# Query loads in 1-KB rows, first casts moved to ScalarE and VectorE, spare transposes in the waits of the ramp, and a new order of work

## The chip, the cores and the metric

One Trainium2 chip, one core of it. The time is device microseconds (us) of the program's execution on that core. A kernel is run several times; medians with the range are given, and a verdict rests on runs of the chip's fast state alone. A ratio is the mean time of one kernel's fast runs over the mean of the other's fast runs in the same rounds on the same chip, so it is not quite the ratio of the two medians that are quoted. In what follows PE is TensorE, DVE is VectorE, ACT is ScalarE, POOL is GpSimd and SP issues most of the DMAs. PSUM holds what TensorE puts out; all other tiles of the kernel lie in SBUF. The ramp is the first part of the run, in which TensorE is not yet full. A string is a row of GpSimd's instructions with no gap between them.

## The reference

Two parts in a row. First linear attention with a decay per head, over blocks of 64 tokens (batch 4, 8 heads, 768 tokens, head size 64). Then a gated MLP whose gate mixes tokens:

```python
for b in range(nb):                                   # 12 blocks of 64 tokens
    intra = einsum('bhic,bhjc->bhij', qb, kb) * Dmask
    out_b = einsum('bhij,bhjd->bhid', intra, vb) + einsum('bhid,bhde->bhie', qb * lam_pow, kv_state)
    kv_state = lam_block * kv_state + einsum('bhsd,bhse->bhde', kb * rev_pow, vb)
x = out as [B, S, H*D]
h = maximum(x @ w_in, 0);  u, v = halves of h
v_n = (v - mean) / sqrt(var + 1e-06)                  # per token
v_s = einsum('ts,bsd->btd', w_spatial, v_n) + b_spatial
out = (u * v_s) @ w_out
```

## The kernel before

The work is cut into 12 tiles of 256 tokens, three to a batch entry. Every tile goes through loads of q, k, v (512-byte rows), casts to bf16 (`kd`, `qc`, `vc`), transposes on TensorE into one PSUM tile `pt` (tiles 0 to 7; later tiles by DMA), copies out of it (`kT` on ScalarE, `qT` on VectorE with the query decay), scores `pam`, a mask `a`, products `pkv` for the state `s`, the output `pat`, and a copy `xT` of it on ScalarE. A batch entry then has `pv` (normalised to `vn` by VectorE), `pu`, `pvs`, `h`, the gate `gT`, and `po`.

Parts that matter here:

```python
    def cast_k(n):
        cast(n, "k", "kd", ldec, nc.gpsimd)
    def cast_v(n):
        s["vc"] = att.tile([P, H, 2, D], BF16, tag="vc", name=f"vc_{n}")
        nc.gpsimd.tensor_copy(out=s["vc"], in_=s["v"])
    def copy_qT(n):
        nc.vector.tensor_tensor(out=transposed(n, "qT"), in0=st[n]["pt"][:, 1],
                                in1=lq[:, n % NR].rearrange("p m g x -> p (m g) x"), op=ALU.mult)
    # ... cut ...
    def copy_x(n):
        # ... cut ...
        nc.scalar.activation(
            out=xT[b][:, r].rearrange("p c g (d m) -> p (c g) m d", m=2),
            in_=st[n]["po"].rearrange("p c g (m d) -> p (c g) m d", m=2), func=AF.Copy)
    # ... cut ...
    def norm(b, r):
        # ... cut ...
        for t in (2 * r, 2 * r + 1):
            nc.vector.tensor_scalar(out=vn[:, t, :], in0=gm["vh", b][:, t, :],
                                    scalar1=mv[:, t, 0:1], scalar2=rstd[:, t:t + 1],
                                    op0=ALU.subtract, op1=ALU.mult)
```

Every engine runs its instructions in the order in which one long string names them. `T:4` is the transposes of tile 4, `vn:1:0` the normalisation of the first pair of token blocks of batch entry 1, `g:0:0` a gate, `cv:6` the cast of v of tile 6, and so on:

```python
    order = """
        q:0 q:1 k:0 k:1 v:0 q:2 k:2 k:3 v:1 v:2 q:3 v:3 ld:0 cq:0 q:4 lq:0 cq:1 lq:1 ck:0 k:4
        lq:2 ck:1 k:5 T:0 qT:0 T:1 kT:0 qT:1 cq:2 kT:1 A:0:0 A:0:1 cv:0 wv v:4 q:5 a:0:0 K:0
        ... (26 further lines)
```

## Time and profile before

| | before |
|---|---|
| time, median of the first 3 runs | 158.95 us (158.13 to 158.96) |
| profiled span | 156.3 us |
| busy: PE, DVE, ACT, POOL | 85%, 60%, 50%, 50% |
| DMA | 51,987 packets, mean 196 GB/s |

The prediction below shows the slices and stretches. What it does not show are three groups that the outcome turns on. These are groups of instructions of the kernel before by line and form: operation, out<-in, sizes, count | busy us in all, mean ns of one | idle time of the engine before them.

```profile
L308 ACT ACTIVATE xT<-pat 128x1024 bf16<-128x1024 f32 x12 | 15.7, 1322 | 9.8 <-PE pat L299 9.8
L352 DVE TENSOR_SCALAR vn<-vh,mv,rstd 128x512 bf16<-128x512 bf16 x24 | 13.3, 596 | 0.4
L205 DVE TENSOR_TENSOR qT<-pt,lq 128x1024 bf16<-128x1024 bf16 x8 | 5.5, 691 | 14.4 <-PE pt L191 9.7 <-ACT kT L202 4.7
```

The mean of `vn` (596 ns) hides two kinds: most take about 410 ns, a few over a microsecond. In the time order of VectorE, a pair of them normally takes 0.73 us, and the longest pair of this kernel 2.42:

```profile
34.56 0.73 DVE L352 TENSOR_SCALAR vn<-vh,mv,rstd 128x512 bf16<-128x512 bf16 x2
41.43 2.42 DVE L352 TENSOR_SCALAR vn<-vh,mv,rstd 128x512 bf16<-128x512 bf16 x2
```

(Start, duration, engine, instruction.) VectorE had begun the second pair and took 1.7 us longer over it, while GpSimd ran a cast of k (`kd`, 41.45 us, 1.93 long). Another pair, at 126.15 us, took 2.12 beside a gate.

### The profile page before, as it was taken

To read this page: it belongs to the slowest core of one execution; us is meant where nothing else is said; L and a number is where in the kernel's file an instruction comes from. 1 tells how busy PE (TensorE), PEld (TensorE's weight loads), DVE (VectorE), ACT (ScalarE), POOL (GpSimd) and SP (SyncE) were. 2 spreads that over 40 slices of the span, in tenths; PEclk is the share of its full clock that TensorE was granted. 3 is DMA by queue.
4 is the path that set the end of the run, shared out by engine and by line. 5 is a ranking of instruction groups with operands and counts; after the bars stand their busy time and mean duration, and the time that the engine had idled before them with its cause. 6 is when DMAs were issued, how large, how long until landed. Compare 5 with 4: busy or idle time off the path is not lost.

```text
span 156.3 us, 4534 instructions
## 1 busy us (share of the span) xinstructions
PE 132.8 (85%) x1992; PEld 88.7 (57%) x1992; DVE 94.0 (60%) x167; ACT 78.0 (50%) x103; POOL 77.7 (50%) x63
## 2 busy tenths in 40 slices
PE   0009469989989999989899999999999999999970
PEld 0008469646868667836665567665665557646440
DVE  1401975696967958656982874787395976424510
ACT  3896234564869423546555033658543376022360
POOL 4076966720359299799802059937220066470000
PEclk9999965999999999999999999999999999999996
DMA  2999999999998999994596995991890011006085
GB/s 43 305 291 290 290 247 295 246 261 212 260 271 260 269 277 204 296 292 124 143 294 115 229 244 125 180 268 31 259 256 33 0 72 66 0 0 268 10 319 208
DMA packets 51987, 30.70 MB, mean 196 GB/s; under 512 B 9472, under 2 KB 48896, under 8 KB 51968
## 3 DMA queue, kind: packets, MB, share of 16 engines
q1 hardware_dynamic: 49312, 27.53, 68.3%
q0 software_dynamic: 2368, 2.75, 10.5%
q8 instruction: 15, 0.25, 0.7%
q10 hardware_dynamic: 288, 0.14, 0.3%
q14 instruction: 4, 0.03, 0.1%
HBM read 24.78 MB, written 6.29 MB: 199 GB/s over the span
## 4 chain that ended last, share of the span: by engine, by line
PE 57%; DMA 16%; SPq 9%; ACT 8%; DVE 4%; POOL 3%; issue 1%; POOLq 0%; ACTq 0%
PE pvs L371 20%; PE po L409 12%; DMA k_in<-in_k_dram 11%; PE pv L325 9%; SPq L72 9%; PE pu L360 8%; DMA v_in<-in_v_dram 5%; ACT wt_sb L461 3%; PE pat L299 2%; ACT vh L330 2%; POOL kd L165 2%; PE pt L191 2%; PE pam L227 1%; ACT kT L202 1%; ACT uT L365 1%
## 5 line engine op out<-in xcount | busy, mean ns | idle before, releaser
L235 DVE TENSOR_TENSOR a<-pam,causal 128x1024 bf16<-128x1024 f32 x24 | 28.7, 1219 | 9.2 <-PE pam L227 9.1
L371 PE MATMUL pvs<-wt_sb,vn 128*128 128x384 bf16 x192 | 32.9, 326 | 0.3 <-ACT wt_sb L461 0.2
L397 POOL TENSOR_TENSOR gT<-h,uT 128x768 bf16<-128x768 f32 x12 | 19.6, 1644 | 21.6 <-PE po L409 16.1
L165 POOL TENSOR_TENSOR kd<-k_in,ldec 128x1024 bf16<-128x1024 f32 x12 | 23.3, 1944 | 12.0 <-DMA k_in<-in_k_dram 11.2
L371 PEld LDWEIGHTS <-vn 128*128 128x128 bf16 x192 | 18.4, 98 | 12.3 <-issue 0.2
L360 PE MATMUL pu<-xT,win_sb 128*128 128x256 bf16 x192 | 22.6, 273 | 0.0
L325 PE MATMUL pv<-win_sb,xT 128*128 128x512 bf16 x96 | 22.3, 380 | 0.0
L386 DVE TENSOR_TENSOR h<-pvs,bsp_bc 128x768 f32<-128x768 f32 (+1 forms) x17 | 15.3, 904 | 11.4 <-PE pvs L371 11.4
L431 ACT ACTIVATE o<-po 128x1024 f32<-128x1024 f32 x11 | 11.3, 1023 | 20.5 <-PE po L409 20.1
L337 DVE BATCH_NORM_STATS2 st<-vh 128x6 f32<-128x512 bf16 x24 | 16.1, 672 | 7.9 <-ACT vh L330 7.9
L178 POOL CAST vc<-v_in 128x1024 bf16<-128x1024 f32 x12 | 12.5, 1044 | 16.7 <-DMA v_in<-in_v_dram 16.7
L308 ACT ACTIVATE xT<-pat 128x1024 bf16<-128x1024 f32 x12 | 15.7, 1322 | 9.8 <-PE pat L299 9.8
L360 PEld LDWEIGHTS <-win_sb 128*128 128x128 bf16 x192 | 18.5, 98 | 3.5 <-issue 0.2
L191 PE MATMUL pt<-ident,kd 128*128 128x128 bf16 x64 | 5.8, 242 | 14.2 <-POOL kd L165 14.2
L330 ACT ACTIVATE vh<-pv 128x1024 bf16<-128x1024 f32 x12 | 12.3, 1023 | 10.0 <-PE pv L325 9.2
L409 PE MATMUL po<-wout_sb,gT 128*128 128x512 bf16 x72 | 16.7, 379 | 0.5 <-DVE s L263 0.5
L365 ACT ACTIVATE uT<-pu 128x1024 bf16<-128x1024 f32 x12 | 12.3, 1024 | 8.9 <-PE pu L360 8.9
L325 PEld LDWEIGHTS <-xT 128*128 128x128 bf16 x96 | 9.0, 98 | 10.2 <-issue 0.2
L202 ACT ACTIVATE kT<-pt 128x1024 bf16<-128x1024 bf16 x8 | 8.2, 1022 | 12.8 <-PE pt L191 10.1
L205 DVE TENSOR_TENSOR qT<-pt,lq 128x1024 bf16<-128x1024 bf16 x8 | 5.5, 691 | 14.4 <-PE pt L191 9.7
L352 DVE TENSOR_SCALAR vn<-vh,mv,rstd 128x512 bf16<-128x512 bf16 x24 | 13.3, 596 | 0.4
L191 PEld LDWEIGHTS <-kd 128*128 128x128 bf16 x64 | 4.6, 109 | 15.6 <-POOL kd L165 14.9
(58 smaller groups left out, 154.3 us busy)
## 6 DMA issues: line engine op xcount, KB each, us to landing
q_in<-in_q_dram SPq DMA_DIRECT2D x12, 512.0 KB, 7.5
k_in<-in_k_dram SPq DMA_DIRECT2D x12, 512.0 KB, 7.4
v_in<-in_v_dram SPq DMA_DIRECT2D x12, 512.0 KB, 7.7
out_dram<-o SPq DMA_DIRECT2D x11, 512.0 KB, 2.8
wsp_raw<-in_moe_w_spatial_dram POOLq DMA_DIRECT2D x1, 1152.0 KB, 13.4
win_sb<-in_moe_w_in_dram POOLq DMA_DIRECT2D x2, 512.0 KB, 9.2
wout_sb<-in_moe_w_out_dram POOLq DMA_DIRECT2D x1, 512.0 KB, 9.0
bsp_bc<-in_moe_b_spatial_dram SPq DMA_DIRECT2D x1, 384.0 KB, 7.4
```

The source lines that it names most:

```text
L72: nc.sync.dma_start(out=t.rearrange("p h m d -> p h (m d)"), in_=src[b, :, r * T2:(r + 1) * T2].rearrange("h (p m) d -> p h (m d)", m=2))
L165: eng.tensor_tensor(out=o, in0=st[n][x], in1=table[:, n % NR].rearrange("p m h -> p h m").unsqueeze(3) .broadcast_to((P, H, 2, D)), op=ALU ...
L235: nc.vector.tensor_tensor(out=s["a"][:, i].rearrange("p h g c x -> p (h g) c x"), in0=s["pam", i].rearrange("p h g c x -> p (h g) c x"), i ...
L308: nc.scalar.activation(out=xT[b][:, r].rearrange("p c g (d m) -> p (c g) m d", m=2), in_=st[n]["po"].rearrange("p c g (m d) -> p (c g) m d ...
L325: nc.tensor.matmul(out=p[:, j], lhsT=xT[b][:, r, j, c, :], rhs=win_sb[:, c, DH:DFF], start=(c == 0), stop=(c == NCH - 1))
L330: nc.scalar.activation(out=vh[:, 2 * r:2 * r + 2, :], in_=ps["v", b, r], func=AF.Relu)
L337: nc.vector.bn_stats(out=st6[:, t, :], in_=vh[:, t, :])
L360: nc.tensor.matmul(out=p[:, f], lhsT=win_sb[:, c, f * P:(f + 1) * P], rhs=xT[b][:, r, :, c, :], start=(c == 0), stop=(c == NCH - 1))
L371: nc.tensor.matmul(out=p[:, i, 0:HW_], lhsT=gm["vn", b][:, s, f * P:(f + 1) * P], rhs=wt_sb[:, s, i * HW_:(i + 1) * HW_], start=(s == 0), ...
L386: nc.vector.tensor_tensor(out=h[:, i], in0=ps["s", b, f][:, i, 0:HW_], in1=bsp_bc.rearrange("p (i x) -> p i x", i=2)[:, i], op=ALU.add)
L397: eng.tensor_tensor(out=gT[:, f, :].rearrange("p (i x) -> p i x", i=2)[:, i], in0=ps["h", b, f][:, i], in1=gm["uT", b][:, f, :].rearrange( ...
L409: nc.tensor.matmul(out=o, lhsT=gT[:, c, t * P:(t + 1) * P], rhs=wout_sb[:, c, f0:f0 + fn], start=(c == 0), stop=(c == NCH - 1))
```

## The change

Its intent: fewer, longer DMA rows for q; the first casts on engines that are free at that time, so that the ramp of about 27 us gets shorter; and transposes of the identity in TensorE's waits, to keep its clock up. A partition now holds 4 tokens of 4 heads of q (p = 2 x group of tokens + half of the heads), so everything that touches q changes its layout: the decay tables, `qT`, the mask's pattern, and the copy `xT`, which now puts tokens back in order with a step of 4. The order string is a new one throughout, not only in the ramp. Cut to its core:

```diff
+    CKD = (0,)
+    CVA = (0, 1, 2)
+    def load_q(n):
+        t = st[n]["q"] = fin.tile([P, 4, 4, D], FP32, tag="q", name=f"q_in_{n}")
+        for f in range(2):
+            nc.sync.dma_start(
+                out=t[f::2].rearrange("p j m d -> p j (m d)"),
+                in_=q[b, 4 * f:4 * f + 4, r * T2:(r + 1) * T2].rearrange(
+                    "j (p m) d -> p j (m d)", m=4))
+    lam_f = const.tile([P, 4], FP32)
+    nc.scalar.dma_start(out=lam_f, in_=lam.rearrange("(f j) -> f j", f=2).unsqueeze(0)
+                        .to_broadcast((D, 2, 4)))
+    nc.scalar.activation(out=loglam_f, in_=lam_f, func=AF.Ln)
... (tables of positions and decays in the new layout: cut)
-        cast(n, "k", "kd", ldec, nc.gpsimd)
+        scaled(n, "k", "kd", ldec, nc.gpsimd if n not in CKD else nc.vector, 2)
-        nc.gpsimd.tensor_copy(out=s["vc"], in_=s["v"])
+        if n in CVA:
+            nc.scalar.activation(out=s["vc"], in_=s["v"], func=AF.Copy)
+        else:
+            nc.gpsimd.tensor_copy(out=s["vc"], in_=s["v"])
+    WARM = {0: 110, 1: 6, 2: 20, 3: 8}
+        for i in range(WARM.get(n, 0)):
+            nc.tensor.transpose(out=pt[:, 0, i % 8, :], in_=ident, identity=ident)
-        nc.vector.tensor_tensor(out=transposed(n, "qT"), in0=st[n]["pt"][:, 1],
-                                in1=lq[:, n % NR].rearrange("p m g x -> p (m g) x"), op=ALU.mult)
+        nc.vector.tensor_tensor(
+            out=transposed(n, "qT").rearrange("p g (f x) -> p g f x", f=2),
+            in0=st[n]["pt"][:, 1].rearrange("p g (x f) -> p g f x", f=2),
+            in1=lq[:, n % NR].rearrange("p m j f x -> p (m j) f x"), op=ALU.mult)
-            out=xT[b][:, r].rearrange("p c g (d m) -> p (c g) m d", m=2),
-            in_=st[n]["po"].rearrange("p c g (m d) -> p (c g) m d", m=2), func=AF.Copy)
+            out=xT[b][:, r].rearrange("p c g (d m) -> p (c g) m d", m=4),
+            in_=st[n]["po"].rearrange("p c g (m d) -> p (c g) m d", m=4), func=AF.Copy)
     order = """
-        q:0 q:1 k:0 k:1 v:0 q:2 k:2 k:3 v:1 v:2 q:3 v:3 ld:0 cq:0 q:4 lq:0 cq:1 lq:1 ck:0 k:4
-        ... (27 further lines)
+        q:0 k:0 q:1 v:0 k:1 q:2 k:2 v:1 k:3 v:2 q:3 v:3 ld:0 lq:0 cq:0 lq:1 ck:0 k:4 q:4 cq:1
+        T:0 lq:2 qT:0 ck:1 k:5 cv:0 v:4 q:5 bsp:0 kT:0 K:0 cq:2 s:0:0 A:0:0 s:0:1 A:0:1 a:0:0
+        ... (7 lines)
+        s:4:1 vh:1:0 pvs:0:0 qT:5 kT:5 bn:1:0 ck:6 pvs:0:1 h:0:0 rs:1:0 vn:1:0 g:0:0 wo pvs:0:2
+        ... (18 further lines)
```

## The prediction

> **What bounds the kernel now.** I read three views in this order: the page's slices (which engine fills up, and when), the busy time by stretch (how much the filled engine loses in each), and the instructions in order of time of the first 45 us (which wait ends last there).
>
> ```profile
> PE   0009469989989999989899999999999999999970
> PEclk9999965999999999999999999999999999999996
> DMA  2999999999998999994596995991890011006085
> ```
>
> A slice is 3.9 us. TensorE (PE) starts at about 12 us, is full from the eighth slice on, and stays full until 4.7 us before the end. The DMA engines are full from the second slice to the seventeenth (to about 66 us). So the run has a ramp of some 27 us, set by loads and by a chain over several engines, and then a long stretch in which TensorE is the bound.
>
> ```profile
> 20.00:28.00 8.00, 7.18 (x188) 6.32 (x189) 5.38 (x8) 3.66 (x5) 5.09 (x5) 0.57 1.20 271
> 43.00:60.00 17.00, 16.34 (x285) 12.06 (x288) 12.06 (x23) 9.37 (x10) 12.31 (x11) 1.00 0.99 269
> 60.00:80.00 20.00, 18.24 (x342) 12.32 (x332) 14.66 (x26) 11.53 (x14) 16.61 (x11) 1.00 0.89 216
> 80.00:100.00 20.00, 19.70 (x310) 13.05 (x309) 12.44 (x21) 7.48 (x10) 9.40 (x7) 1.00 0.94 182
> 100.00:120.00 20.00, 20.00 (x268) 11.98 (x267) 13.87 (x29) 11.31 (x15) 7.90 (x5) 1.00 0.73 187
> ```
>
> The columns are the stretch, its length, busy us of TensorE, its weight loads, VectorE, ScalarE and GpSimd, then the granted clock, DMA share and GB/s. From 43 to 120 us TensorE idles 0.66 + 1.76 + 0.30 + 0 = 2.7 us. That, and the ramp, is all there is to win; the matmuls themselves are not changed. In 20 to 28 us the clock is 0.57: second by second it is 0.50 from 20.3 to 27.7 us, so what runs there runs at half speed.
>
> ```profile
> 9.81 3.82 POOL L165 TENSOR_TENSOR kd<-k_in,ldec 128x1024 bf16<-128x1024 f32 x2 [0.82 <-ACT lq L127]
> 13.07 0.20 ACT L133 ACTIVATE sq_t<-eps_t 128x1 f32<-128x1 f32 x1
> 14.52 1.02 ACT L202 ACTIVATE kT<-pt 128x1024 bf16<-128x1024 bf16 x1 [1.25 <-DVE qT L205]
> 15.59 1.07 PE L227 MATMUL pam<-qT,kT 64*64 64x128 bf16 x32
> 20.05 0.62 PE L191 MATMUL pt<-ident,kd 128*128 128x128 bf16 x8 [1.93 <-POOL kd L165]
> 43.43 0.62 PE L191 MATMUL pt<-ident,kd 128*128 128x128 bf16 x8 [0.47 <-POOL kd L165]
> ```
>
> The first scores (pam) start at 15.59 us, after two casts of k in a row on GpSimd, the transposes, and the kT copy on ScalarE, which itself is busy until 13.27 with decay tables. The transposes of tile 4 at 43.43 end the ramp. Their k was on the wait list as 8.8 us of waiting by GpSimd, but TensorE stood for only half a microsecond: it had pu matmuls to do until 42.96. So the long DMA wait in the chain is nearly hidden already.
>
> **What the Trainium skill says.** "DMA: Bandwidth & Descriptors", section "Why small descriptors are slow (HBM only)", names a fixed cost per packet. The trace agrees in kind: 512-byte loads saturate at 290 GB/s, 28.2 ns a row on each of 16 engines; an output store with 2-KB rows (128 to 130 us) moves 0.524 MB in 2 x 0.71 = 1.42 us of share, 369 GB/s, 88.8 ns a row. "VectorE: DVE Perf Modes", section "Mode 2x_1P", wants 16-bit operands with step 1 for two results a cycle. The trace agrees: qT from bf16 takes 0.69 us for 1024 elements, the mask from f32 1.22 us. "TensorE: Matmul & The Clock Gate", Part 1, says that an idle window of some 3.4 us halves the clock and as long a busy one restores it; here the half clock lasts 7.4 us and ends after nearly continuous work from 23.9 to 27.7 us. Its Part 4 says that transposes do not count as such work; no run here shows it yet.
>
> **The change, part by part.**
>
> q in 1-KB rows. A line through the two row times above gives 8 ns + 0.0395 ns per byte, so 48.5 ns for 1 KB (an estimate), and a q load takes 32 x 48.5 = 1.55 us instead of 64 x 28.2 = 1.81. That is 0.25 us each: 1.25 us by tile 4, 2.0 us by tile 7. On the path it is worth something only where DMA ends a wait, which above was half a microsecond. It costs: the qT copy now reads PSUM with a step of 2, so I expect the mask's 1.22 us and not 0.69, eight times, 4.2 us more on VectorE, 1.6 of it in tiles 1 to 3. The xT copy on ScalarE writes with step 4 instead of 2; it takes 1.32 us now, against 1.02 for a dense copy, and I leave it at 1.3 with a risk of 1.6 to 1.9. Scores of the last four tiles read qT with step 2; I count nothing.
>
> Loads reordered (q0 k0 q1 v0 k1) and casts moved. k0 is second instead of third: 9.8 - 1.8 - 0.25, about 7.7 us. Its cast moves to VectorE at the mask's 1.22 us, done near 9.0, so the transposes of tile 0 are ready 2.8 us earlier than 11.8. But ScalarE sets the first scores now: its tables ended at 13.27, it gets a second logarithm and one more DMA issue (0.2 + up to 0.4), then the new cast of v0 (1.05), then kT (1.02): 13.27 + 0.4 + 1.05 + 1.02 = 15.75. The scores start at about 15.8 instead of 15.6. So the early k buys nothing at that point; it only lets the kv products and state 0 (s, two instructions of 0.42 us) come first.
>
> Spare transposes, 144 in all. The 110 before tile 0 begin when the identity is ready, near 3.0 us. Cold they take 0.10 us (8 in 0.82 at 11.80), warm 0.05. Warm after 5 us: 50 cold and 60 warm, 8 us, done at 11 us, harmless beside ScalarE's 15.8. All cold: 11 us, done at 14, and the scores slip to some 17. The other 34 cost 34 x 0.055 = 1.9 us of TensorE in the ramp, partly in its waits. What they buy is the clock. From 20.3 to 27.7 TensorE was busy for about 6.5 us at half clock; a part of that is latency of short matmuls, so I take 2 us as what the cold clock cost.
>
> The walk to tile 4. After 15.8 VectorE has, up to the last mask of tile 3: 8 masks x 1.22, 3 qT x 1.22, 5 states x 0.42, sum 15.5 us with hardly a gap, so the last mask ends near 32.4 (38.0 before). TensorE follows it, then runs dense from about 30.7: pv of three parts 5.2, kv and inter products 0.8, pu of three parts 5.25, intra 0.6, transposes of tile 4 with q 1.0, together 12.9, so it ends that set at 43.6. Before, the same set ended at 44.5. Gain 0.9 us. Reading it the other way, as losses in the ramp: before 3.3 us idle from 16 to 27 us, 2 cold, 1.3 idle later, 6.6 in all; after 2.7 idle and 1.9 spare, 4.6; minus tile 1's transposes, which now come after 16 us, 0.9. Gain 1.1. The tables of weights and k4, q4 should be there: the spatial weights are asked for only after v3 is cast, and k4 now stands ahead of q4.
>
> The rest. The order of everything after tile 4 is new as well. Of the 2.7 us that TensorE idles from 43 to 120 I count half as saved: GpSimd, which is 16.6 of 20 us busy in 60 to 80 us, has four casts fewer to do (1.94 + 3 x 1.04 = 5.1 us) ahead of that stretch, so it should run earlier. That is 1.3 us. The end, 4.7 us after the last matmul, stays.
>
> Sum: 1.0 + 1.3 = 2.3 us off 158.95, **156.6 us**, rounded to 156.5.
>
> **The rivals.**
> First, VectorE becomes the bound of the ramp, or more of one than I count (qT at 1.22, states before masks), and the gain there is eaten: time 158.0 to 159.0. For it speaks that VectorE is 27.3 of 48 us busy now and dense for 16 us in my walk; against it, that TensorE has pu and pv matmuls to fill with later.
> Second, the clock is worth more than 2 us and the re-ordered loads let TensorE be dense from 27 instead of 30.7: up to 3.5 us more, time 153.0. For it speaks the 0.57 clock; against it, that the first half of the input weights lands only at about 27 us, as before.
> Third, the transposes do not warm the clock, 110 of them run cold and hold up tile 0: first scores near 17 us, time 158.5. For it speaks that tiles 0 and 1 ran 3.8 us of transposes from 11.8 us on and were still at 0.10 us each; against it, that a window may simply not have ended.
> Fourth, the copy xT at step 4 takes 1.9 us: 7 us more on ScalarE. It is half idle, so under 1 us on the time.
>
> **Range and chances.** The ramp is 1.0 with some 1.5 either way, the rest 1.3 with 1.0 either way, and both rivals of gain and loss are live: 153.8 to 158.6 us. Faster by over 2% means under 155.8 us. The sum is 0.7 us short of it, with a spread of about 1.8, so a third by the arithmetic; as an author who tunes would hardly keep four edits for nothing, I put 0.39. Slower by over 2% would need a lasting new wait on TensorE: 0.03.
>
> **What would show it.** Right: q loads paced at 1.5 to 1.6 us; qT at 1.22 us with 1.0 unchanged for kT; first scores at 15.5 to 16.2 us behind ScalarE; clock 1.0 from 20 to 28 us; the last mask of tile 3 done at 31 to 34 us; the pu and transposes of tile 4 done at 42 to 44 us; under 2 us of TensorE idle from 43 to 120. Wrong: a clock under 0.8 in the ramp; TensorE waiting for kd or qc of tile 4 for over 1 us; xT near 1.9 us; more TensorE idle in 60 to 80 us than 1.8.

## The result, and the profile after

| | before | after |
|---|---|---|
| time, median of 4 runs | 158.54 us (157.47 to 158.96) | 176.04 us (175.2 to 177.28) |
| ratio of the fast runs | 1 | 1.1121, interval 1.1028 to 1.1215 |
| profiled span | 156.3 us | 173.9 us |
| DMA packets | 51,987 | 46,181 |

The changed kernel is 11% slower, 17.5 us. The result is correct. The slices of the page after (40 slices of 4.3 us; busy tenths, granted clock tenths, DMA share):

```profile
PE   3981856759996999079799999999999998999980
PEclk9999688987999999859999999999999999999996
DMA  2799799999999999800000599999830600032066
```

TensorE has a hole in the seventeenth slice (about 70 to 74 us), with the clock at half right behind it; in the five slices after it (74 to 96 us) DMA is idle. The ramp lasts longer too: full slices begin only with the tenth, at 39 us. The stretches that the prediction showed for before read, after (busy us of PE, its weight loads, DVE, ACT and POOL, then clock, DMA share, GB/s):

```profile
20.00:28.00 8.00, 5.63 (x95) 5.20 (x97) 3.48 (x3) 2.24 (x4) 4.37 (x4) 0.73 1.03 246
43.00:60.00 17.00, 15.46 (x204) 11.85 (x205) 12.06 (x26) 11.84 (x15) 6.98 (x5) 1.00 1.09 314
60.00:80.00 20.00, 14.39 (x189) 9.00 (x188) 15.39 (x16) 7.33 (x7) 10.52 (x8) 0.83 0.69 164
80.00:100.00 20.00, 18.94 (x317) 13.15 (x318) 13.56 (x25) 14.29 (x15) 12.15 (x8) 1.00 0.12 35
100.00:120.00 20.00, 19.89 (x399) 12.96 (x400) 17.48 (x26) 10.45 (x11) 13.67 (x9) 1.00 1.10 252
```

From 43 to 120 us TensorE idles 1.54 + 5.61 + 1.06 + 0.11 = 8.3 us, where it idled 2.7, and a part of the rest ran at a lower clock. In the ramp VectorE does less in the same time than before (3.48 us of 8, not 5.38): it waits. The instructions that answer to those of the prediction, in time order:

```profile
6.81 0.21 ACT L124 ACTIVATE loglam_f<-lam_f 128x4 f32<-128x4 f32 x1 [3.07 <-DMA lam_f<-in_lam_dram]
9.56 1.23 DVE L196 TENSOR_TENSOR kd<-k_in,ldec 128x1024 bf16<-128x1024 f32 x1 [1.20 <-DMA k_in<-in_k_dram]
15.53 0.20 ACT L164 ACTIVATE sq_t<-eps_t 128x1 f32<-128x1 f32 x1
16.59 1.00 ACT L243 ACTIVATE kT<-pt 128x1024 bf16<-128x1024 bf16 x1
17.64 1.07 PE L275 MATMUL pam<-qT,kT 64*64 64x128 bf16 x32 [0.47 <-ACT kT L243]
28.95 1.22 DVE L246 TENSOR_TENSOR qT<-pt,lq 128x1024 bf16<-128x1024 bf16 x1 [3.23 <-ACT kT L243]
50.65 0.61 PE L232 MATMUL pt<-ident,kd 128*128 128x128 bf16 x8
```

ScalarE waits 3.07 us for a 2-KB load of the decay in 16-byte rows, which took 5.63 us from its issue at 1.16; so its tables end at 15.73 instead of 13.27, and the first scores start at 17.64 instead of 15.59. The third `qT` waits 3.23 us for ScalarE, and tile 4 starts 7.2 us later than before. The groups:

```profile
L356 ACT ACTIVATE xT<-pat 128x1024 bf16<-128x1024 f32 x12 | 29.6, 2468 | 17.7 <-PE pat L347 17.7
L400 DVE TENSOR_SCALAR vn<-vh,mv,rstd 128x512 bf16<-128x512 bf16 x24 | 18.1, 796 | 0.4
L246 DVE TENSOR_TENSOR qT<-pt,lq 128x1024 bf16<-128x1024 bf16 x8 | 9.8, 1224 | 13.6 <-ACT kT L243 12.0 <-PE pt L232 1.5
```

The copy `xT` went from 1322 to 2468 ns; `qT` went from 691 to 1224, as foreseen. And this is the hole, VectorE, GpSimd and TensorE in time order:

```profile
66.59 7.46 DVE L400 TENSOR_SCALAR vn<-vh,mv,rstd 128x512 bf16<-128x512 bf16 x2
66.63 1.64 POOL L445 TENSOR_TENSOR gT<-h,uT 128x768 bf16<-128x768 f32 x1 [12.61 <-DVE rstd L398]
68.21 0.80 POOL L184 DMA_DIRECT2D wout_sb<-in_moe_w_out_dram  x1
69.01 1.05 POOL L194 CAST qc<-q_in 128x1024 bf16<-128x1024 f32 x1
69.99 1.04 POOL L212 CAST vc<-v_in 128x1024 bf16<-128x1024 f32 x1
71.00 1.93 POOL L196 TENSOR_TENSOR kd<-k_in,ldec 128x1024 bf16<-128x1024 f32 x1
72.87 1.03 POOL L212 CAST vc<-v_in 128x1024 bf16<-128x1024 f32 x1
74.98 0.48 PE L298 MATMUL pkv<-vc,kd 64*64 64x64 bf16 x10 [5.61 <-DVE h L434]
```

Two `vn` instructions that need 0.73 us took 7.46, from just before GpSimd's string of six back-to-back instructions began until it ended at 73.90. The first of them got through when the gate ended (68.3 us); the second took 5.72, over the DMA issue and all four casts. VectorE's `h` behind them came late, no PSUM tile came free, and TensorE stood for 5.6 us; then it worked at a granted clock of 0.60 from 75 to 80 us.

### The profile page after: what moved, and what is told of

It is laid out like the page before. It is cut to its first block, busy times and chain, and to the rows that moved or that the text cites. A ratio compares the mean times of both kernels' runs of the same rounds, so it can differ in the third digit from the quotient of the medians.

```text
span 173.9 us, 4832 instructions
## 1 busy us (share of the span) xinstructions
PE 144.9 (83%) x2123; PEld 99.4 (57%) x2136; DVE 105.5 (61%) x174; ACT 93.4 (54%) x106; POOL 72.9 (42%) x61
## 2 busy tenths in 40 slices
DMA packets 46181, 30.72 MB, mean 177 GB/s; under 512 B 9808, under 2 KB 43088, under 8 KB 46160
## 4 chain that ended last, share of the span: by engine, by line
PE 63%; ACT 18%; DVE 12%; DMA 3%; issue 1%; ACTq 0%
PE pvs L419 15%; PE pv L373 12%; PE po L457 12%; PE pu L408 9%; ACT xT L356 6%; DVE vn L400 4%; PE pt L232 4%; DVE qT L246 4%; ACT kT L243 3%; DMA lam_f<-in_lam_dram 3%; ACT lq L159 3%; PE pat L347 3%; PE pam L275 3%; PE pkv L298 2%; PE pt L227 2%; DVE a L283 1%
## 5 line engine op out<-in xcount | busy, mean ns | idle before, releaser
L356 ACT ACTIVATE xT<-pat 128x1024 bf16<-128x1024 f32 x12 | 29.6, 2468 | 17.7 <-PE pat L347 17.7
L419 PE MATMUL pvs<-wt_sb,vn 128*128 128x384 bf16 x192 | 34.3, 335 | 0.2
L196 POOL TENSOR_TENSOR kd<-k_in,ldec 128x1024 bf16<-128x1024 f32 x11 | 21.2, 1931 | 9.7 <-DMA k_in<-in_k_dram 9.6
L373 PE MATMUL pv<-win_sb,xT 128*128 128x512 bf16 x87 | 22.9, 391 | 1.2 <-ACT rstd L391 0.5
L479 ACT ACTIVATE o<-po 128x1024 f32<-128x1024 f32 x11 | 11.2, 1023 | 14.3 <-PE po L457 13.7
L400 DVE TENSOR_SCALAR vn<-vh,mv,rstd 128x512 bf16<-128x512 bf16 x24 | 18.1, 796 | 0.4
L246 DVE TENSOR_TENSOR qT<-pt,lq 128x1024 bf16<-128x1024 bf16 x8 | 9.8, 1224 | 13.6 <-ACT kT L243 12.0
L275 PE MATMUL pam<-qT,kT 64*64 64x128 bf16 x384 | 10.6, 230 | 7.2 <-DVE qT L246 4.9
L298 PE MATMUL pkv<-vc,kd 64*64 64x64 bf16 x320 | 5.6, 197 | 10.7 <-DVE h L434 5.6
L227 PE MATMUL pt<-ident 128*128 128x128 bf16 x144 | 11.9, 259 | 2.9 <-POOL ident masks.py:199 2.9
L194 POOL CAST qc<-q_in 128x1024 bf16<-128x1024 f32 x7 | 7.3, 1039 | 15.2 <-DMA q_in<-in_q_dram 15.2
```

Of the source, the lines that this page charges most:

```text
L196: eng.tensor_tensor(out=o, in0=st[n][x], in1=table[:, n % NR].rearrange("p m h -> p h m").unsqueeze(3) .broadcast_to((P, 16 // M, M, D)), ...
L246: nc.vector.tensor_tensor(out=transposed(n, "qT").rearrange("p g (f x) -> p g f x", f=2), in0=st[n]["pt"][:, 1].rearrange("p g (x f) -> p ...
L275: nc.tensor.matmul(out=pam[half(c), hh, g2, m, :], lhsT=s["kT"][half(hh), m * NG + g, half(c)], rhs=qblk(n, g, hh, c), start=True, stop=True)
L356: nc.scalar.activation(out=xT[b][:, r].rearrange("p c g (d m) -> p (c g) m d", m=4), in_=st[n]["po"].rearrange("p c g (m d) -> p (c g) m d ...
L373: nc.tensor.matmul(out=p[:, j], lhsT=xT[b][:, r, j, c, :], rhs=win_sb[:, c, DH:DFF], start=(c == 0), stop=(c == NCH - 1))
L419: nc.tensor.matmul(out=p[:, i, 0:HW_], lhsT=gm["vn", b][:, s, f * P:(f + 1) * P], rhs=wt_sb[:, s, i * HW_:(i + 1) * HW_], start=(s == 0), ...
```

## The experiments

Eighteen kernels ran, each beside runs of the kernel before on the same chip (medians of those 158.4 to 158.9 us). Theories at the start: **the order** made the loss (new collisions, above all the hole), or **the content** did (ScalarE's longer copy and later tables, spare transposes, `qT`).

### One suspect at a time, out of the changed kernel

**e1, the stalled `vn` before the `h` that opens the gate**, so that it runs before GpSimd's string:

```diff
-  ... pvs:0:1 h:0:0 rs:1:0 vn:1:0 g:0:0 wo pvs:0:2
+  ... pvs:0:1 rs:1:0 vn:1:0 h:0:0 g:0:0 wo pvs:0:2
```

> One swap in the order: the normalisation of tile pair 1:0 (vn, two VectorE instructions) stands before the first bias add h:0:0 instead of after it, so that GpSimd's string (gate, q cast, v cast, k cast, v cast) starts after vn and not beside it. Theory A (vn, which reads and writes SBUF in a fast mode, is held off while GpSimd runs back to back: 7.46 us for a pair that takes 0.74 elsewhere): the pair takes under 1 us, TensorE's gap of 5.6 us from 69.4 to 75.0 goes and with it the half clock to 78, time down 5.5 to 7 us, to about 169.5. Rival B (the gap is from PSUM buffers or ScalarE's long xT copies, vn is only beside it): vn is short but a gap of 3 us or more stays near there, time down by less than 2 us.

Measured: 173.09 us (172.15 to 174.23), ratio 1.0890, correct. The hole is gone, and the transposes of tile 6 start at 72.26 instead of 79.63 us. But the next pair ran into GpSimd's next string, which filled 75.5 to 90.8 us (VectorE's time order):

```profile
85.70 5.60 DVE L400 TENSOR_SCALAR vn<-vh,mv,rstd 128x512 bf16<-128x512 bf16 x2
```

It follows that the stall belongs to the pair's place beside GpSimd's work, not to the pair itself, and that moving one pair only moves the problem: of 7.4 us won, 3 to 4 were left at the end.

**e2, no load of `lam_f`**; the second column is worked out from the first on VectorE:

```diff
-    nc.scalar.dma_start(out=lam_f, in_=lam.rearrange("(f j) -> f j", f=2) ...)
-    nc.scalar.activation(out=loglam_f, in_=lam_f, func=AF.Ln)
+    nc.vector.tensor_tensor(out=loglam_f, in0=loglam[:, 4:8], in1=loglam[:, 0:4], op=ALU.subtract)
+    nc.vector.tensor_scalar(out=loglam_f, in0=loglam_f, scalar1=par, scalar2=None, op0=ALU.mult)
+    nc.vector.tensor_tensor(out=loglam_f, in0=loglam_f, in1=loglam[:, 0:4], op=ALU.add)
```

(`par` is 0 or 1 there, by the partition's parity.)

> The second load of lam (lam_f, landed at 6.8 us) and its logarithm are dropped; the same values come from loglam by three small VectorE instructions. Correct result. Theory A (ScalarE's tables waited 3.1 us for lam_f and the chain to the first scores hangs on ScalarE): tables end at 13.2 to 13.5 instead of 15.7, first scores at 15.2 to 15.7 instead of 17.6, time down 1.5 to 2.5 us. Rival B (k of tile 1, landed at 16.25, and the later loads set the ramp): first scores earlier, but tile 1 and what follows where they were, time down under 0.7 us. Also open: the DMA engines' idle 1.5 us from 3.9 to 5.5 us; if lam_f made it, the first q lands near 6.1 us instead of 7.7.

Measured: 171.39 us (170.64 to 173.56), ratio 1.0744, correct. The first scores start at 14.39 us, 3.2 us earlier, and tile 4 at 48.88 instead of 50.65. Three of the four timed runs are fast; the fourth (173.56 us) is the one that was profiled, so only marks of the ramp are read from it. The gain, 4.7 us by the medians and 6.0 by the ratios, is over twice the 1.5 to 2.5 that was expected; the ramp's marks show 1.8 of it, and no fast profile shows the rest. The question that the expectation left open has an answer in the traces: from 4 to 5 us the DMA engines' share is 0.08 in the changed kernel and 0.79 here, and the first cast of q starts at 7.66 and at 6.06 us. So it is in every run: 0.07 to 0.46 and 7.2 to 8.3 us with the load of `lam_f`, 0.79 to 1.11 and 6.0 to 6.1 without. The small load held up the others too.

**e3, `xT` with a write step of 2** (wrong: tokens land in the wrong order):

```diff
-            out=... "p c g (d m) -> p (c g) m d", m=4),  in_=... "p c g (m d) -> p (c g) m d", m=4)
+            out=... "p c g (d m) -> p (c g) m d", m=2),  in_=... "p c g (m d) -> p (c g) m d", m=2)
```

> The xT copy on ScalarE writes with step 2 as before the change (tokens then stand in a wrong order: the result is wrong on purpose), all else is the changed kernel. xT should take 1.32 us instead of 2.47. Theory A (the 12 x 1.15 us on ScalarE stand in the path, since kT and qT of the next tile wait behind xT in the ramp): time down 4 to 6 us. Rival B (ScalarE is 54% busy and only the ramp's two or three xT count): down 1 to 2.5 us.

Measured: 173.21 us (172.79 to 173.96), ratio 1.0879. One copy takes 1324 ns again. The gain (2.8 us by the medians, 3.8 by the ratios) lies between the two theories.

**e4, no spare transposes**:

```diff
-    WARM = {0: 110, 1: 6, 2: 20, 3: 8}
+    WARM = {}
```

> The 144 spare transposes are dropped, all else is the changed kernel. Theory A (they stand in TensorE's queue ahead of the tile's own transposes, 20 of them at half clock took 2.07 us ahead of tile 2, and they don't keep the clock up: it was 0.5 at 17.8 to 20.5, 24.5 to 27.6): first scores unchanged at 17.6, time down 1 to 3 us, mean clock within 0.03. Rival B (they do hold the clock, without them it is 0.5 for longer): time up 1 to 3 us, more than 6 us at 0.5 between 15 and 35 us.

Measured: 175.56 us (174.2 to 177.63), ratio 1.0993, correct; its interval (1.0899 to 1.1087) overlaps the changed kernel's, so by itself this is not shown to gain. Tile 4 starts 2.7 us earlier (47.91) and tile 7 still 2.8 (92.91 against 95.71), but the last matmul ends only 0.7 us earlier (168.36 against 169.09): most of what the ramp won is given back after tile 7. Without the spare transposes, the eight of tile 0 take 1.03 us, with them 0.61. So the 110 do warm the clock, as their own count in four stretches of the changed kernel shows (busy us and count of PE and of the weight loads):

```profile
3.00:5.00 2.00, 2.00 (x20) 2.00 (x21) 1.00 0.34 108
5.00:7.00 2.00, 2.00 (x22) 2.00 (x20) 1.00 0.73 201
7.00:9.00 2.00, 2.00 (x36) 2.00 (x34) 1.00 1.12 337
9.00:11.00 2.00, 2.00 (x40) 2.00 (x38) 1.00 1.16 316
```

Twenty in 2 us at first, forty from some 7 us on. (The clock, the column that reads 1.00, shows nothing of this.) But TensorE then waits from 12.2 to 16.7 us for ScalarE, its first scores come at 17.64, and the eight of tile 1 at 19.26 take 1.06 us, cold again. The warmth was gone before there was work for it.

**e7, a dense `xT`**: the write is contiguous, and the step (32 f32 values) is in the read from PSUM:

```diff
-            out=... "p c g (d m) -> p (c g) m d", m=4),  in_=... "p c g (m d) -> p (c g) m d", m=4)
+            out=... "p c g (d m) -> p (c g) d m", m=4),  in_=... "p c g (m d) -> p (c g) d m", m=4)
```

> The changed kernel, but xT is written densely and the permutation stands on the PSUM side of the copy (read with a step of 32 f32). Correct result. If ScalarE pays for steps on the written side only: 1.0 to 1.1 us a copy instead of 2.47, and the time falls as with step 2 (1.32 us), by 2.5 to 4 us. If it pays for steps on the read side as well: 2 us or more a copy and no gain.

Measured: 173.35 us (172.86 to 176.19), ratio 1.0917, correct. One copy takes 1023 ns, as a copy without any step does:

```profile
L356 ACT ACTIVATE xT<-pat 128x1024 bf16<-128x1024 f32 x12 | 12.3, 1023 | 17.5 <-PE pat L347 17.5
```

So ScalarE pays for the step of its bf16 write (1: 1.02 us, 2: 1.32, 4: 2.47) and not for that of its f32 read. Yet 17 us less on ScalarE gave only some 3 us here (2.7 by the medians, 3.2 by the ratios); the stall of 7.46 us is still there.

### Order and content apart

**e5, the changed content with the old order**, and **e6, the old content with the new order** (the order strings swapped, nothing else), e5 from the changed kernel and e6 from the one before:

```diff
-  q:0 k:0 q:1 v:0 k:1 q:2 k:2 v:1 ...        e5: 28 lines of the changed order out
+  q:0 q:1 k:0 k:1 v:0 q:2 k:2 k:3 ...        e5: 28 lines of the old order in;  e6: the reverse
```

> The changed kernel's code (q rows, lam_f, xT at step 4, casts of v0 to v2 on ScalarE and of k0 on VectorE, spare transposes) with the old order of work. Theory A (the new order lost most: it puts vn beside GpSimd's strings and pv, pu later in the ramp): 160.5 to 165 us, no vn over 2.5 us, no TensorE gap over 2 us after 45 us. Rival B (the content of the change lost most: lam_f, xT, qT, spare transposes): 168 us or more.

> The kernel before, with the new order of work and nothing else changed. Theory A (order): 165 to 171 us, with a vn of 5 us or more and TensorE idle for over 4 us about it. Rival B (content): 157 to 161 us.

Measured: e5 170.70 us (170.67 to 170.78), ratio 1.0764; e6 169.43 (167.78 to 169.68), ratio 1.0661; both correct. Both theories hold: the order alone costs 6.6%, the content alone 7.6%, both together 11.2%, less than the sum. In e6 tile 4 starts at 43.7 us, as in the kernel before: the new order costs nothing up to there. A pair of `vn` takes 7.46 us again, at 57.83. In e5 no pair is over 3.04; TensorE there waits for ScalarE (`seen`, `vc`, `xT`, 2.5 to 2.8 us each).

**e8, the old order, without the `lam_f` load (as e2) and without spare transposes (as e4)**:

```diff
-    WARM = {0: 110, 1: 6, 2: 20, 3: 8}
+    WARM = {}
-    nc.scalar.dma_start(out=lam_f, ...)               and the further lines of e2
-  q:0 k:0 q:1 v:0 k:1 q:2 k:2 v:1 ...
+  q:0 q:1 k:0 k:1 v:0 q:2 k:2 k:3 ...
```

> As the changed code with the old order, also without the second load of lam and without spare transposes; q rows, qT at step 2, xT at step 4 and the moved casts stay. Theory A (order, lam_f and spare transposes are the loss, the rest is small): 157.5 to 161 us. Rival B (xT at 2.47 us and qT at 1.22 us cost most by themselves): 163 us or more.

Measured: 166.83 us (166.45 to 168.84), ratio 1.0545, correct. 3.5 us less than e5, and still 8 us behind the kernel before. TensorE's waits name what is left (engine, line, waited for: us in all, times, longest; the wait of 11.1 us for the first transposes is left out):

```profile
PE pv L372 <- ACT xT L355: 3.1, 3, 1.6
PE pam L274 <- ACT seen L333: 2.5, 2, 1.6
PE pkv L297 <- ACT vc L209: 2.5, 1, 2.5
```

**e9, e8 with the dense `xT` of e7**, and **e10, e9 with all casts of v and k back on GpSimd** (`CVA = ()`, `CKD = ()`), so that only q in 1-KB rows and the step-2 `qT` remain of the change:

> The lean kernel of before (old order, second decay column worked out on VectorE, no spare transposes) with the copy xT written densely (1.02 us instead of 2.47). What is left of the change: q in 1-KB rows, qT read with a step of 2, first casts of v on ScalarE and of k on VectorE. Theory A (ScalarE carries the rest of the loss, the step-4 copy for most of it): 160.5 to 163.5 us, the waits of TensorE for xT go from 3.1 us to under 1.5. Theory B (the moved casts and qT set the rest): 165 to 167, little changed. Correct result.

> As the run beside it, and the casts of v 0 to 2 and k 0 are back on GpSimd: of the whole change only q in 1-KB rows stays, with the step-2 copy qT. Theory A (casts were neutral and cost ScalarE in the ramp): 158 to 160.5 us, 1.5 to 3 us under the run beside it, T of tile 4 back at 43.5 to 45 us. Theory B (GpSimd is the scarce engine and the casts helped): equal to the run beside it or slower. If q rows are worth their 1.0 us of ramp as predicted, it falls at or under 158.5. Correct result.

Measured: e9 158.58 us (158.55 to 159.79), ratio 1.0031 (0.9985 to 1.0076); e10 159.40 (158.66 to 160.24), ratio 1.0059 (1.0017 to 1.0100); both correct. The whole of the 8 us was the write step of `xT`, more than either theory gave it. The moved casts are neutral: the two intervals overlap. And the q rows, all else cured, bring nothing: 0.6% slower, if anything. Where `xT` costs its 8 us can be followed by the starts of transposes, e8 against e9: tile 4 at 46.90 and 43.17 us, tile 7 at 76.04 and 71.29, the last matmul's end at 160.23 and 152.32. The copy lies between `pat` and the `pv` and `pu` that read it, and in the old order TensorE has nothing else to fill with in several of these places (its waits for `xT`, 4.4 us in e8, are gone in e9).

**e11, the kernel before with only a dense `xT`** (the edit of e7, with m=2):

> The kernel before with one edit: the copy xT is written densely and reads PSUM with the step (1.02 us instead of 1.32, 3.6 us off ScalarE in all). ScalarE is not the bound: within 1% of before, 157.3 to 159.2 us. A rival: copies sit on the path between intra products and pv in the ramp, so 1 to 2 us off. Correct result.

Measured: 158.77 us (158.41 to 159.39), ratio 1.0022 (0.9991 to 1.0052), correct. 0.3 us more or less per copy is not felt; 1.45 us is.

### The stall of `vn`

The Trainium skill, "SBUF — State Buffer", section "Who interferes with whom", says that VectorE in its two-port modes and GpSimd contend for a shared pair of ports, which is a lock: the first to issue has it "for the whole instruction". `vn` (a `tensor_scalar` on bf16 in SBUF) can use such a mode. The rival was that the pair waits for something else that the string holds.

**e12, `vn` with a step of 2** in and out, to leave the fast modes:

```diff
-  out=vn[:, t, :],  in0=gm["vh", b][:, t, :]
+  out=vn[:, t, :].rearrange("p (x e) -> p e x", e=2),  in0=gm["vh", b][:, t, :].rearrange("p (x e) -> p e x", e=2)
```

> The changed kernel, and the normalisation vn walks its row in two interleaved halves (step 2 in and out, same numbers), which should take it out of VectorE's fast modes. If the 7.46 us of two vn instructions is the lock between VectorE's fast mode and GpSimd, no vn pair is over 2 us any more though each takes 0.5 to 0.7 us, TensorE no longer stands from 69.4 to 75 us, and the time falls by 4 to 7 us, to 168 to 172. If it waited for something else (a semaphore, GpSimd's own data), it stays at 7 us and the time at 175 to 178. Correct result.

Measured: 175.95 us (175.25 to 177.02), ratio 1.1107, correct; the pair at 66.15 us takes 7.63. By its letter the expectation refutes the lock. But the edit need not have done what it was meant to: `vn` went from 412 to 580 ns (median), and the skill's "VectorE: DVE Perf Modes", section "Mode 2×_2P", asks for no step of one in that two-port mode. So the run told nothing of the ports, and another form was needed.

**e13, `vn` also writes a sum of each row** (`accum_out`), a form that the same SBUF section excludes from the two-port modes:

```diff
-                                    op0=ALU.subtract, op1=ALU.mult)
+                                    op0=ALU.subtract, op1=ALU.mult, accum_out=acc[:, t:t + 1])
```

> The changed kernel, and the normalisation vn also writes out a sum per row, which the Trainium skill (SBUF — State Buffer, section Who interferes with whom) says never enters the two-port modes[...]. One vn should take 0.55 to 0.8 us. Lock theory: no pair is over 2.2 us, TensorE no longer stands at 69 to 75 us, 168 to 173 us in all. Rival (vn waits for something that GpSimd's string holds, whatever the port): a pair of 7 us stays and the time stays at 175 to 178. The sum may change the meaning of the second operation, so a wrong result is possible and is accepted.

Measured: 167.54 us (166.85 to 169.95), ratio 1.0572, correct: 8.5 us off by making 24 instructions twice as slow. The tile's own view gives min/median/max ns, first and last start:

```profile
L401 DVE TENSOR_SCALAR_CACHE_REDUCE vn<-vh,mv,rstd x24: 802/805/806, 46.1 to 142.5; 128x512 bf16<-128x512 bf16 x24
```

In the changed kernel the same view reads 401/412/5717. All 24 now take the same time, beside the same string of GpSimd or not, and TensorE is busy 5.00 of 5 us from 65 to 70 and 4.64 from 70 to 75, where it had 4.37 and 0.02. The order string and the inputs of `vn` are the same, and it starts beside the same gate as before (65.29 us, the gate at 65.33). A wait for data would have stayed. So it is the plain form of `vn` beside GpSimd that costs the 7 us; that ports are what it waits for rests on the skill.

How long a `vn` is held is another matter. In e9 a pair starts beside a string of five instructions, the start of which is shown here, and takes 3.18 us:

```profile
43.07 3.18 DVE L399 TENSOR_SCALAR vn<-vh,mv,rstd 128x512 bf16<-128x512 bf16 x2
43.12 1.04 POOL L211 CAST vc<-v_in 128x1024 bf16<-128x1024 f32 x1 [5.63 <-DMA v_in<-in_v_dram]
44.12 1.98 POOL L195 TENSOR_TENSOR kd<-k_in,ldec 128x1024 bf16<-128x1024 f32 x1
46.04 1.10 POOL L193 CAST qc<-q_in 128x1024 bf16<-128x1024 f32 x1
```

It ended at 46.25 us, soon after `kd`, and not with the string at 50.1. So a place beside a string need not cost the whole string. What makes VectorE be passed over several times, as in the hole and in e1, is not shown.

**e14, e6 with this `vn`** (old content, new order), and **e15, the kernel before with this `vn`**:

> The kernel before with the order of the changed one (169.43 us) and vn in the same one-port form. Lock theory: the two long stalls go and the time falls to 161 to 165; if all that the order cost was the lock, to 160. Rival: over 168.

> The kernel before with only vn in the one-port form. Its pairs took at most 2.42 us in the fast form. If the lock costs the kernel before little: within 1% of it, 157.5 to 160. If these short stalls are on the path: 1 to 2 us off.

Measured: e14 161.71 us (161.24 to 162.44), ratio 1.0209 (1.0179 to 1.0238); e15 158.02 (157.35 to 159.01), ratio 0.9977 (0.9935 to 1.0019); both correct. Of the 6.6% of the new order, 4.5 are the lock and 2.1 are left. The kernel before loses nothing measurable to it: its held pairs take 2.42 us at most. That they lie where TensorE has other work fits and was not tested.

**e16, everything cured but the order stays new**: e9's content, the changed order, this `vn`:

> The changed kernel with everything cured that the runs have found: dense copy xT, second decay column worked out on VectorE, no spare transposes, vn in the one-port form; the order, the 1-KB rows of q and the moved casts stay. If the causes found are all there are: 157 to 161 us, no slower than 161. If the order has another cost of its own (pv and pu come later, copies of kT before qT): 162 to 166.

Measured: 162.05 us (161.41 to 162.68), ratio 1.0226 (1.0195 to 1.0257), correct: above the 161 that was set as the bound for "the causes found are all there are", and just inside the 162 to 166 of the other theory. So the order has a cost of its own, some 2%. What it is was not taken apart. In e14 and e16 GpSimd is busy 20.00 of the 20 us from 60 to 80 (17.75 in e15), and TensorE is busy 18.07 and 18.36 us from 80 to 100, where e15 has 19.59; that points at the strings of casts, and is a reading, not a test.

**e17, the changed kernel with this `vn` and the dense `xT`**, and **e18, the kernel before with both**:

> The changed kernel with vn in the one-port form (167.54 us) and the dense copy xT. In the changed order the dense copy alone gave 2 to 3 us, in the old order 8. If its gain was hidden behind the two long stalls of vn: 161 to 164 us, 4 to 6 us off. If the changed order simply does not lean on xT: 165 to 166.5.

> The kernel before with both cures, one-port vn and dense xT, each within half a per cent alone. TensorE is full; within 1% of before, 157 to 159.5 us; faster by over 1% would mean that the short stalls add up.

Measured: e17 164.26 us (164.10 to 165.65), ratio 1.0383, correct: 3.0 us under e13, between the two theories and short of the 4 to 6 that hiding would give. With the stalls gone the step-4 copy is worth as much in the new order (3 us) as with them, while it is 8 us in the old one: the new order puts the first `pv` later (33 to 38 us in e6, e16 and e17, and 27 to 28 in the kernel before, e8 and e9) and may so lean on `xT` less, which fits and was not tested. e18: 158.15 us (156.88 to 158.53), ratio 0.9964 (0.9928 to 1.0001), correct: the same as the kernel before within 1%. No version that ran is shown to beat it.

## Why the prediction was wrong, point by point

The predicted 156.5 us was 19.5 off, well outside its range, and slower by over 2% had been given 0.03. From the changed kernel down, the ratios give a sum in the new order (1% is 1.585 us):

| step | from | to | us |
|---|---|---|---|
| `vn` held up by GpSimd (e13) | 1.1121 | 1.0572 | 8.7 |
| step-4 write of `xT` (e17) | 1.0572 | 1.0383 | 3.0 |
| `lam_f` load and spare transposes (e16) | 1.0383 | 1.0226 | 2.5 |
| layout of q, moved casts (e14) | 1.0226 | 1.0209 | 0.3 |
| the order itself (e15) | 1.0209 | 0.9977 | 3.7 |

The steps depend on their sequence: in the old order `xT` is 8 us and the lock nothing. The 0.3 us is within the noise, as the intervals of e14 and e16 overlap.

- **"The rest", minus 1.3 us, is the step that failed.** It took the new order after tile 4 on trust, as relief of GpSimd, and counted its freed time as TensorE's gain. GpSimd's busy time did fall (77.7 to 72.9 us), but the new order packed its casts and gates into strings, and the pairs of `vn` beside two of them were held for 7.46 us (the changed kernel) and 5.60 (e1). This term came out as +8.7 us of lock and +3.7 of the order's own instead of -1.3. The warning in the profile before was the pairs of 2.42 and 2.12 us beside GpSimd's work.
- **Rival four had the right mechanism and the wrong size.** It named `xT` at step 4 with 1.9 us and under 1 us on the time, since ScalarE is half idle. It takes 2.47 us, and its place between `pat` and `pv` counts, not ScalarE's share: 3 us in the new order, 8 in the old one.
- **First scores at 15.8 us behind ScalarE**: the right engine, 17.64 in fact. The missing 1.9 us is the load of `lam_f`, costed as 0.2 of logarithm and 0.4 of issue; its landing, 5.63 us after issue, was not asked for. e2 brings the scores to 14.39.
- **The ramp, minus 1.0 us, failed at the walk of VectorE.** The last mask of tile 3 ended at 40.66 us, not 32.4. The sum of VectorE's durations was right (`qT` 1.22 us, masks 1.22), but "with hardly a gap" was not: `qT` of tiles 1 to 3 waits 7.7 us for `kT` (2.67, 3.23 and 1.76). For tiles 1 and 2, ScalarE itself stood idle for 7.1 us before `kT`, waiting for TensorE's transposes, which stand in line behind the spare ones; for tile 3 a copy `xT` of 2.47 us came first. The transposes of tile 4, which were to be done at 43.6, began at 50.65. The spare transposes put off the tile's own at tiles 1 to 3 by 2.9 us (0.62 + 1.86 + 0.44, start to start), not 1.9, as 26 of the 34 took 0.10 us each; without them (e4) tile 4 starts 2.7 us earlier.
- **Spare transposes warm, done at 11 us: right** (11.32), and useless. They bought no clock: from 20 to 28 us it was 0.73, not 1.0. Rival three, that transposes do not warm, is refuted.
- **q rows: the transfer got cheaper, about as predicted.** From 8 to 16 us, with DMA full, the engines moved 291 GB/s before and 306 in e10; 0.25 us off every third load of 1.81 us would make 305. The prediction said that DMA hardly ends a wait on the path, and e10 agrees: no gain at all.
- **Readings that were off.** The half clock before lasts 6.8 us (20.6 to 27.4), not 7.4, and DMA is full to the eighteenth slice (70 us). The first k was to be there at 7.7 us; its cast waited for it until 9.56. And 15.8 + 15.5 is 31.3: the 1.1 us up to 32.4 are not accounted for (the first scores take 1.07). None of this decides the outcome.
- **Rival one, VectorE as the bound of the ramp**: no; it was idle there more than before, waiting for `kT`. **Rival two, 153 us**: no.
- **The chances** leaned on the author's likely success ("an author who tunes would hardly keep four edits for nothing"). No profile line stood behind that.

## What to carry to other kernels

An order string is a change of its own, and its cost cannot be read from the work it moves: after a reorder look at each engine's longest instruction against its median, and ask what ran on the other engines meanwhile. An instruction on VectorE that GpSimd can hold up is better placed in GpSimd's gaps, or given a slower form that is not held; slower by 0.4 us each, it made the changed kernel 8.5 us faster. And a copy between two matmul groups is costed by its place in the chain, not by how idle its engine is; put the step into the read from PSUM rather than into the bf16 write (1.02 us for a copy, against 1.32 or 2.47).

## What the Trainium skill lacked or had wrong

- "SBUF — State Buffer", section "Who interferes with whom": it gives the lock to the first comer "for the whole instruction". In e9 that is so: each `vn` of a pair got through at the end of one instruction of GpSimd, with the next right behind it (3.18 us in all). But one `vn` of 0.41 us was held 5.72 us in the changed kernel, through a DMA issue and four casts in a row (68.3 to 74.1 us), and in e1 a pair took 5.60 us, to the end of a string. The skill does not say when the waiting side is passed over between back-to-back instructions, and the runs don't show what decides it. That the form with a sum stays out of it agrees: 802 to 806 ns in all 24.
- The same page, section "Specifications (TRN2)": full bandwidth needs two or more hits in a 16-byte line, and each new line costs a penalty of a size not given. For ScalarE's bf16 writes two hits were not enough: a copy of 128x1024 took 1.02 us at step 1, 1.32 at step 2 and 2.47 at step 4, which is two elements to such a line. Its f32 read of PSUM at a step of 32 values cost nothing (1.023 us).
- "TensorE: Matmul & The Clock Gate", Part 4: it says that transposes do not count as work for the clock. Here 110 transposes in a row went from 0.10 to 0.05 us each after some 4 us.
- The clock column of the profile reads 1.00 from 3 to 7 us of the changed kernel, though its transposes took 0.10 us each there; no page was found that speaks of this column at the start of a run. The durations tell.
- No page was found that gives the latency of small broadcast loads, or says that they hold up others: 2 KB in 16-byte rows landed 5.63 us after issue, 4 KB in 32-byte rows 2.8 (3.6 in the kernel before); with the first of them the DMA engines' share from 4 to 5 us was 0.07 to 0.46, without it 0.79 to 1.11.
